# Turning C and a quarter of x by VectorE and transfers instead of TensorE, in a gated mix of an S5 layer and an FFN

## The chip, the cores and the metric

One core of a Trainium2 chip. The metric is the device time of one execution in microseconds (us), the median of several runs. Engines are called TensorE (PE in the profile), VectorE (DVE), ScalarE (ACT), GpSimd (POOL) and SyncE (SP); SP issues most transfers.

## What is computed

x is one sequence of 2048 tokens of 448 features, in bf16. Out of it come an S5 state space layer `a` and a dense FFN `b`, mixed by a gate of each token. `x = A_x` feeds both.

```
g    = sigmoid((x * gate_w).sum(-1))
a:     Lam_bar = exp(dt * Lam);  B_bar = ((Lam_bar - 1) / Lam) * Bmat        # complex, 448 states
       Bu = x @ B_bar.T;   h[t] = Lam_bar * h[t-1] + Bu[t]
       a  = 2 * real(h @ Cmat.T) + x * Dskip
b:     b  = silu(x @ w1) @ w2                                                # 448 -> 1792 -> 448
out  = g * a + (1 - g) * b
```

## The kernel before

**Tiling.** The 2048 tokens are worked on in four chunks `tc` of 512 (CH), each of four token tiles `tb` of 128. The 448 complex states are 896 real rows, held as 7 slots of 128 (slots 0 to 2 and the lower half of slot 3 real, the rest imaginary). The names of the products in the lists of work are:

- F(tc): x times w1, 14 tiles of 128 columns for each chunk; ScalarE applies silu while it copies PSUM to `aT` (L634).
- B(tc): x times B, 7 tiles for each chunk, copied out of PSUM to `U` (`UG`), by VectorE in the first chunk (L640) and by ScalarE in the others (L642).
- G(tb): the second FFN product, 14 matmuls (L774); ScalarE scales by 1 - g into `fe` (L780), and a GpSimd transfer adds that to `Tb` in SBUF (L782). `Tb` is `xnat` itself, in which x times Dskip times g already lies (L849).
- C(tb): the readout of 7 matmuls, state `H` times scaled `CP` (L795). VectorE computes g * product + `Tb` (L798), SP stores it (L801).

F and B (L663) run as pairs of 64-row matmuls, side by side, with one bank pair of PSUM for each pair of tiles; there are four bank pairs. They need x and B with features on partitions. x comes in with tokens on partitions (`xnat`) and is turned by TensorE with an identity matrix: `x0_transposes` for chunk 0 (L478), `x_transposes` for chunks 1 to 3 (32 small matmuls each, L508, copied out of PSUM at L516 and L518). B is turned in the same way (`b_transposes`, L604). C is loaded to `Cnat` (which shares its memory with H2), turned by TensorE in four groups (`readout_weights`, L814) and scaled out of PSUM by ScalarE (L822, L825) and VectorE (L827, L830) into `CP`.

**The recurrence** (`lanes(tc)`). VectorE rotates U by COS and SIN into `H` (A) with the help of `PI`, scans the seven slots (`tensor_tensor_scan`, L736) into the f32 buffer `Gf`, and rotates back into H with the help of `PO`. Between, `Gf` is cast to bf16 in `U` again, by GpSimd transfers (L390) in chunks 0 to 2 and by ScalarE in chunk 3 (L746). In chunk 0 the first rotation is 18 small operations, in the others four large ones (L729 to L732). There are two `UG`, one `PI`, `PO` and `Gf`, and four `H`.

**The order.** Operations are put into a `Plan`. TensorE's order is the one in which they are added: the last lines of the function write it out by hand. Every other engine's order comes from a list scheduler (`order`, L104): of the operations that could start earliest by its own costs it takes the one with the lowest `prio`. Loads are reckoned at 300 KB per us in the order of their queue (`RATE`, L60). The order is fixed when the kernel is built; on the chip each engine works through its list, and an instruction that waits holds up everything behind it on that engine. TensorE's list:

```
F0 (8 tiles), B0, F0 (6), B1; parameters, turning of B and of x chunk 1 in between
cp(0) G(0,1) cp(1,2) G(2,3) cp(3)
F1, F2 (1 tile), B2; x chunk 2 turned in between
G(4..7) C(0..3)
F2 (13), B3, F3; x chunk 3 turned in between
C(4..7) G(8..11) C(8..11) G(12..15) C(12..15)
```

**Loads.** SP issues x chunk 0, w1, the parameters, B, the last part of w1, gate_w and Dskip, x chunk 1, w2, C in eight pieces, and x chunks 2 and 3 (L401 to L441).

Of the kernel before, what the change touches and what calls it, by code (L numbers as in the profile page):

```python
# [7 lines left out]
ALU = mybir.AluOpType  # L8
# [6 lines left out]
S_TOK = 2048  # L15
# [9 lines left out]
NFILL = 2  # L25
XCOL = [0, 128, 256, 320]
# [22 lines left out]
class Op:  # L49
    __slots__ = ("i", "eng", "fn", "reads", "writes", "cost", "prio", "sem",  # L50
                 "deps", "succ", "ps_w", "ps_r", "start", "end", "bytes", "tag", "own")


class Plan:
# [5 lines left out]
    RATE = {"pool": 300e3, "hw": 300e3}  # L60
    LAP = {"dve": 0.08, "act": 0.09}
# [6 lines left out]
    def add(self, eng, fn, reads=(), writes=(), cost=0.2, prio=50, sem=None, nbytes=0, tag=""):  # L68
# [28 lines left out]
        o.own = False  # L97
        o.start = o.end = None
# [5 lines left out]
    def order(self):  # L104
# [14 lines left out]
        def earliest(o):  # L119
            t = 0.0  # L120
# [23 lines left out]
        while len(done) < len(ops):  # L144
# [5 lines left out]
            for eng, lst in cands.items():  # L150
# [9 lines left out]
                o = min((c for c in cand if c[0] <= t0 + 1e-9), key=lambda c: (c[1].prio, c[1].i))[1]  # L160
# [116 lines left out]
def bass_gated_mix__ssm_conv_s5__dense_activation_silu__prompt_kernel(nc, A_x, A_Lambda_re, A_Lambda_im, A_B_re, A_B_im, A_C_re, A_C_im,  # L277
               A_log_dt, A_Dskip, B_x, B_w1, B_w2, gate_w, out):
    with ExitStack() as ctx:
# [9 lines left out]
        xT = sb("xT", [128, 4, S_TOK], BF16)  # L289
# [3 lines left out]
        CP = sb("CP", [128, NSLOT, D_MOD], BF16)  # L293
        aT = [sb(f"aT{k}", [128, NFB, CH], BF16) for k in range(2)]
        UG = [sb(f"UG{k}", [128, 8, CH], BF16) for k in range(2)]
# [3 lines left out]
        H2C = sb("H2C", [128, 3840], BF16)  # L299
        H = [H2C[:, 0:3584].rearrange("p (s n) -> p s n", s=NSLOT) if k == 2 else sb(f"H{k}", [128, NSLOT, CH], BF16) for k in range(4)]  # L300
        Cnat = H2C[:, :].rearrange("p (b l) -> p b l", b=4)
        cnn = [f"H2_{s}" for s in range(7)] + ["H2_3i"]
# [91 lines left out]
        def load_w1(q, k, a, b):  # L394

            cols = slice(w1cuts[k], w1cuts[k + 1])
            src = B_w1[320:448, cols] if a == 3 else B_w1[128 * a:128 * b, cols].rearrange("(b p) f -> p b f", p=128)
            load(q, w1s[:, 3, cols] if a == 3 else w1s[:, a:b, cols], src, " ".join(f"w1_{k}_{i}" for i in range(a, b)),
                 256 * (b - a) * (cols.stop - cols.start))
# [11 lines left out]
        Bnat = H[3][:, :, 0:D_MOD]  # L411
        load("sp", Bnat[:, 0:3, :], A_B_re[0:384, :].rearrange("(b p) d -> p b d", p=128), "H3_0 H3_1 H3_2", 384 * 896)
        load("sp", Bnat[0:64, 3, :], A_B_re[384:448, :], "H3_3", 64 * 896)
        load("sp", Bnat[64:128, 3, :], A_B_im[384:448, :], "H3_3i", 64 * 896)
        load("sp", Bnat[:, 4:7, :], A_B_im[0:384, :].rearrange("(b p) d -> p b d", p=128), "H3_4 H3_5 H3_6", 384 * 896)
        btn = {s: [f"BT{s}_{h}" for h in range(2)] for s in range(7)}
        load_w1("sp", len(w1cuts) - 2, 0, 3)
        load_w1("sp", len(w1cuts) - 2, 3, 4)
# [8 lines left out]
        def load_C():  # L427

            for h in range(2):
                rows = lambda a: a[224 * h:224 * h + 224, :].rearrange("(b p) l -> p b l", p=56)  # L430
                to = Cnat[64 * h:64 * h + 56]
                load("sp", to[:, :, 0:448], rows(A_C_re), f"Cn0{h} " + (" ".join(cnn) if h == 0 else ""), 224 * 896)
                load("sp", to[:, :, 576:960], rows(A_C_im[:, 0:384]), f"Cn1{h}", 224 * 768)
                load("sp", to[:, :, 448:512], rows(A_C_im[:, 384:448]), f"Cn2{h}", 224 * 300)
                load("sp", to[:, :, 512:576], rows(A_C_re[:, 384:448]), f"Cn3{h}", 224 * 300)
# [32 lines left out]
        def x0_transposes(q0, part, who):  # L468
# [12 lines left out]
            for h in range(2):  # L481
                src = lambda h=h: bk(tk, h).bitcast(BF16)[:, 0:256].rearrange("p (q b n) -> p q b n", q=2, n=64)
                dst = xT[:, q0:q0 + 2, 256 * part:256 * part + 256].rearrange("p q (b h n) -> p q b h n", h=2, n=64)[:, :, :, h, :]
# [11 lines left out]
        xn_of = {tc: {q: [f"xT{tc}_{h}" for h in range(2)] for q in range(4)} for tc in range(1, NCH)}  # L495
        xn_of[0] = {q: [f"xT0_{q}{part}{h}" for part in range(2) for h in range(2)] for q in range(4)}

        def x_transposes(tc, who):
# [13 lines left out]
            for h in range(2):  # L512
                src = lambda h=h: bk(tk, h).bitcast(BF16).rearrange("p (q b n) -> p q b n", q=4, b=4)
                dst = xT[:, :, tc * CH:(tc + 1) * CH].rearrange("p q (b h n) -> p q b h n", h=2, n=64)[:, :, :, h, :]
                if who[h] == "d":
                    DVE(lambda e, src=src, dst=dst: e.tensor_copy(dst, src()), [tk], [f"xT{tc}_{h}"], 0.69, 2.2, "xTe")  # L516
                else:
                    ACT(lambda e, src=src, dst=dst: e.activation(dst, src(), AF.Copy), [tk], [f"xT{tc}_{h}"], act_cost(1024), 2.2, "xTe")  # L518

# [73 lines left out]
        def b_transposes(s0, s1, who):  # L593
# [12 lines left out]
            PE(mm, [f"H3_{s}" for s in range(s0, s1)] + ["H3_3i"] * (s0 <= 3 < s1) + ["ident"], [tk], n * 4 * 0.0285, "BT")  # L606
# [16 lines left out]
        def evict(pair, tk):  # L623

            kinds = [t[0] for t in pair]
            for k, n in ((0, 2),) if pair[0][:2] == pair[-1][:2] and len(pair) == 2 else ((0, 1), (1, 1))[:len(pair)]:
# [10 lines left out]
                U, un = UG[tc % 2], f"U{tc % 2}_"  # L637
                dst = U[:, sl, :]
                if tc == 0:
                    DVE(lambda e, src=src, dst=dst: e.tensor_copy(dst, src()), [tk], [f"{un}{m}" for m in names], 0.15 + 0.53 * n, 2.6, "U")  # L640
                else:
                    ACT(lambda e, src=src, dst=dst: e.activation(dst, src(), AF.Copy), [tk], [f"{un}{m}" for m in names], act_cost(512 * n), 5, "U")  # L642
# [4 lines left out]
        def x_products(tiles, fill={}, wait=()):  # L647
# [10 lines left out]
            def steps(k, h, a, z):  # L658
                def body(pe):
                    for n, cut in list(enumerate(part[h]))[a:z]:  # L660
                        for b, ((i, p0), tile) in enumerate(zip(cut, pairs[k])):
                            tc = tile[1]
                            r = pe.matmul(bk(toks[k], b), weights(tile, p0, p0 + 64, i), xT[p0:p0 + 64, i, tc * CH:(tc + 1) * CH],  # L663
# [42 lines left out]
        def lanes(tc):  # L706
            pr = 20 + tc
            A, an = H[tc], f"H{tc}"
            U, u = UG[tc % 2], f"U{tc % 2}_"
            Gb = U  # L710
            t = f"L{tc}"
            if tc == 0:
# [20 lines left out]
            for s in (3, 0, 4, 1, 5, 2, 6) if tc else (0, 4, 1, 5, 2, 6, 3):  # L733
# [8 lines left out]
                for dst, src, name in cuts:  # L742
                    if tc + 1 < NCH:
                        load("pool", dst, src, name, 180000, 1, [f"Gf{s}"])
# [23 lines left out]
        def ffn2(tb):  # L768
# [13 lines left out]
            P.add("pool", lambda e: e.dma_start(Tb[:, tb, :], f[:, :], accum_op=ALU.add), [fn, f"Tb{tb}"], [f"Tb{tb}"], 0.94, 2, sem(), 115000, tag="Tb+")  # L782

        outs = [sem() for _ in range(NOT)]

        def readout(tb):
# [3 lines left out]
            for n, (a, b) in enumerate(cuts):  # L790
                tk = Ps()

                def mm(pe, tk=tk, a=a, b=b):
                    for s in range(NSLOT):
                        r = pe.matmul(bk(tk)[:, 0:b - a], H[tc][:, s, o:o + 128], CP[:, s, a:b], start=(s == 0), stop=(s == NSLOT - 1))  # L795
                    return r
                PE(mm, [f"H{tc}_{s}" for s in range(7)] + [f"CP{s}" for s in range(NSLOT)], [tk], NSLOT * (0.0025 + (b - a) / 2400), f"C{tc}")
# [5 lines left out]

        def readout_weights(k):

            tk = Ps(2)

            def mm(pe):
                for j, c0 in ((0, 128 * k), (1, 448 if k == 3 else 576 + 128 * k)):
                    for b in range(4):  # L810
                        o = j * 224 + 56 * b
                        for h in range(2):
                            p = slice(64 * h, 64 * h + 56)
                            r = pe.transpose(bk(tk, h).bitcast(BF16)[:, o:o + 56], Cnat[p, b, c0:c0 + 128], ident[p, p])  # L814
                return r
            PE(mm, [f"Cn{n}{h}" for n in range(4) for h in range(2)] + cnn + ["ident"], [tk], 8 * 0.0285, "CT")
# [102 lines left out]
```

## Time and profile before

| what | value |
|---|---|
| median of 3 runs (lowest, highest) | 141.22 us (141.2, 141.76) |
| the profiled execution | 141.25 us, its span 139.5 us |
| granted TensorE clock | 0.998 |
| TensorE busy, matmuls | 135.9 us (97%), 1201 |
| VectorE busy | 122.0 us (87%) |
| ScalarE busy | 90.3 us (65%) |
| GpSimd busy | 39.2 us (28%) |
| read from HBM, written | 7.17 MB, 1.84 MB |

The span is the time from the first to the last instruction in the trace; the difference to the execution's time lies around it. Times in timelines are microseconds from the span's start, then the duration. A row of the chain gives start, length, engine, tile, line of the kernel and number of instructions. A row of the groups gives line, engine, operation, result and operands with shape, count, then busy time and mean duration in ns, then the idle time ahead of it. A row of the windows gives a stretch, its length, the busy time of TensorE's matmuls and weight loads, VectorE, ScalarE and GpSimd in it, each with its number of instructions, then the clock, the busy share of the 16 DMA engines and GB/s.

### The profile page before, as it was taken

How to read it: one execution, taken by the hardware profiler on the slowest of the kernel's cores; microseconds unless marked ns; L12 is line 12 of the kernel's file. 1: busy time of each engine (PE TensorE's matmuls, PEld its weight loads, DVE VectorE, ACT ScalarE, POOL GpSimd, SP SyncE). 2: the span in 40 equal slices, each digit the busy share in tenths (PEclk: the TensorE clock that was granted, in tenths of full speed). 3: DMA queues.
4: the chain of work that ended last, by engine and by line, in shares of the span. 5: the costliest groups of instructions: out<-in, count | busy, mean ns of one | idle time of the engine just before them, and what ended most of it. 6: DMA issues, size and time to landing. Idle time of an engine off the chain costs nothing.

```text
span 139.5 us, 3000 instructions
## 1 busy us (share of the span) xinstructions
PE 135.9 (97%) x1201; PEld 67.0 (48%) x1201; DVE 122.0 (87%) x179; ACT 90.3 (65%) x157; POOL 39.2 (28%) x72
## 2 busy tenths in 40 slices
PE   7999999999999999999999999999999999999992
PEld 2445454455544544455544544444455555555561
DVE  0319999999999999999999999999999999997053
ACT  3349768999989999823694887799931268312300
POOL 7134040100248440227733001824000314022220
PEclk9999999999999999999999999999999999999999
DMA  4998999510156770104976200674202322323242
GB/s 136 337 294 243 363 320 238 177 42 0 31 79 94 129 110 1 38 15 73 157 131 155 38 5 0 95 133 79 38 4 97 66 33 36 83 83 61 40 94 71
DMA packets 17956, 14.71 MB, mean 105 GB/s; under 512 B 2835, under 2 KB 17814, under 8 KB 17942
## 3 DMA queue, kind: packets, MB, share of 16 engines
q0 software_dynamic: 6064, 5.51, 24.8%
q1 hardware_dynamic: 11318, 8.65, 20.7%
q10 hardware_dynamic: 560, 0.36, 0.8%
q8 instruction: 9, 0.15, 0.4%
q14 instruction: 5, 0.04, 0.1%
HBM read 7.17 MB, written 1.84 MB: 65 GB/s over the span
## 4 chain that ended last, share of the span: by engine, by line
PE 97%; DVE 0%; issue 0%
PE ps L663 46%; PE ps L774 31%; PE ps L795 15%; PE ps L463 2%; PE ps L508 1%; PE ps L478 1%; PE ps L814 1%; PE ps L604 1%; DVE ot L798 0%; PE ps L675 0%; PE ps L464 0%; PE ps L536 0%
## 5 line engine op out<-in xcount | busy, mean ns | idle before, releaser
L663 PE MATMUL ps<-xT,w1s 64*128 64x512 bf16 x392 | 48.5, 378 | 0.0
L774 PE MATMUL ps<-w2s,aT 128*128 128x448 bf16 x224 | 43.2, 353 | 0.0
L634 ACT ACTIVATE aT<-ps 128x1024 bf16<-128x1024 f32 (+1 forms) x30 | 28.7, 969 | 8.5 <-PE ps L663 8.4
L774 PEld LDWEIGHTS ps<-w2s,aT 128*128 128x128 bf16 x224 | 21.7, 98 | 20.4 <-ACT xnat L849 0.4
L663 PEld LDWEIGHTS ps<-xT,w1s 64*128 64x128 bf16 x392 | 19.7, 94 | 22.3 <-DVE xT L486 0.7
L663 PE MATMUL ps<-xT,BT 64*128 64x512 bf16 x196 | 25.8, 376 | 0.0
L782 POOL DMA_DIRECT2D xnat<-fe x16 | 14.1, 900 | 37.9 <-ACT fe L780 37.2
L780 ACT ACTIVATE fe<-ps,g 128x448 bf16<-128x448 f32 x16 | 10.1, 632 | 21.1 <-PE ps L774 21.0
L390 POOL DMA_DIRECT2D UG<-Gf x27 | 14.7, 549 | 20.9 <-DVE Gf L736 20.4
L736 DVE TENSOR_TENSOR_SCAN Gf<-rc,gin,H 128x512 f32<-128x512 f32 x14 | 17.2, 1268 | 0.0
L795 PE MATMUL ps<-CP,H 128*128 128x448 bf16 (+2 forms) x98 | 16.4, 326 | 0.0
L663 PEld LDWEIGHTS ps<-xT,BT 64*128 64x128 bf16 x196 | 10.8, 94 | 11.1 <-DVE Gf L562 0.2
L798 DVE SCALAR_TENSOR_TENSOR ot<-ps,g,xnat 128x448 bf16<-128x448 f32 (+2 forms) x18 | 10.8, 622 | 6.0 <-issue 4.6
L390 POOL DMA_DIRECT2D UG<-UG x8 | 4.8, 597 | 29.2 <-ACT UG L642 17.4
L704 DVE TENSOR_TENSOR H<-UG,COS 128x3584 bf16<-128x3584 bf16 (+4 forms) x10 | 12.6, 1266 | 0.0
L795 PEld LDWEIGHTS ps<-CP,H 128*128 128x128 bf16 x98 | 8.9, 98 | 7.5 <-DVE k L752 0.4
L642 ACT ACTIVATE UG<-ps 128x1024 bf16<-128x1024 f32 (+1 forms) x12 | 10.7, 923 | 1.4 <-PE ps L663 1.4
L842 ACT ACTIVATE junk<-xg 128x448 bf16<-128x448 bf16 x16 | 9.2, 574 | 2.1 <-DVE xg L704 2.0
L849 ACT ACTIVATE xnat<-xnat,g 128x448 bf16<-128x448 bf16 x16 | 9.8, 671 | 0.2
L704 DVE TENSOR_TENSOR PI<-UG,SIN 128x512 bf16<-128x512 bf16 (+2 forms) x13 | 9.1, 722 | 0.0
L704 DVE TENSOR_TENSOR PO<-UG,SIN 128x1536 bf16<-128x1536 bf16 (+1 forms) x8 | 8.7, 1087 | 0.1
L736 DVE TENSOR_TENSOR_SCAN Gf<-rc,gin,H2C 128x512 f32<-128x512 f32 x7 | 8.5, 1265 | 0.0
(102 smaller groups left out, 126.5 us busy)
## 6 DMA issues: line engine op xcount, KB each, us to landing
UG<-Gf POOLq DMA_DIRECT2D x21, 128.0 KB, 2.5
xnat<-fe POOLq DMA_DIRECT2D x16, 112.0 KB, 2.6
out_dram<-ot SPq DMA_DIRECT2D x15, 112.0 KB, 1.7
w2s<-in_B_w_dram SPq DMA_DIRECT2D x1, 1568.0 KB, 11.8
xnat<-in_A_x_dram SPq DMA_DIRECT2D x3, 448.0 KB, 6.1
w1s<-in_B_w_dram SPq DMA_DIRECT2D x1, 576.0 KB, 6.2
UG<-UG POOLq DMA_DIRECT2D x8, 64.0 KB, 2.2
H2C<-in_A_C_re_dram SPq DMA_DIRECT2D x2, 196.0 KB
```

The source lines that it names most:

```text
L390: P.add(q, lambda e: e.dma_start(dst, src), list(after), name.split(), 0.6 if q == "pool" else 0.5, prio, sem(), nbytes, tag="ld " + name)
L634: ACT(lambda e, src=src, dst=dst: e.activation(dst, src(), AF.Silu), [tk, "tbl"], [f"aT{tc % 2}_{m}" for m in names], act_cost(512 * n), 2 ...
L642: ACT(lambda e, src=src, dst=dst: e.activation(dst, src(), AF.Copy), [tk], [f"{un}{m}" for m in names], act_cost(512 * n), 5, "U")
L663: r = pe.matmul(bk(toks[k], b), weights(tile, p0, p0 + 64, i), xT[p0:p0 + 64, i, tc * CH:(tc + 1) * CH], start=(h == 0 and n == 0), stop=( ...
L704: DVE(lambda e: e.tensor_tensor(o, a, b, op), r, w, dve_cost(n, 2), prio, tag)
L736: DVE(lambda e, s=s, b=b, init=init: e.tensor_tensor_scan(Gf[:, s, :], rc[:, b:b + 1].to_broadcast([128, CH]), A[:, s, :], init, ALU.mult, ...
L774: r = pe.matmul(bk(tk)[:, 0:D_MOD], aT[tc % 2][:, fb, o:o + 128], w2s[:, fb, :], start=(fb == 0), stop=(fb == NFB - 1))
L780: ACT(lambda e: e.activation(f[:, :], bk(tk)[:, 0:D_MOD], AF.Copy, scale=g1[:, tb:tb + 1]), [tk, f"g1_{tc}"], [fn], act_cost(448, 1), 7, "fe")
L782: P.add("pool", lambda e: e.dma_start(Tb[:, tb, :], f[:, :], accum_op=ALU.add), [fn, f"Tb{tb}"], [f"Tb{tb}"], 0.94, 2, sem(), 115000, tag= ...
L795: r = pe.matmul(bk(tk)[:, 0:b - a], H[tc][:, s, o:o + 128], CP[:, s, a:b], start=(s == 0), stop=(s == NSLOT - 1))
L798: DVE(lambda e, tk=tk, a=a, b=b: e.scalar_tensor_tensor(ot[tb % NOT][:, a:b], bk(tk)[:, 0:b - a], g[:, tb:tb + 1], Tb[:, tb, a:b], ALU.mul ...
L849: ACT(lambda e, tb=tb: e.activation(Tb[:, tb, :], xnat[:, tb, :], AF.Copy, scale=g[:, tb:tb + 1]), [f"xd{tc}", f"g_{tc}"], [f"Tb{tb}"], ac ...
```

## The change

- **C** is loaded ahead of w2 instead of behind it, in six pieces, with rows in plain order (128 x 3 and 64 x 1); GpSimd clears the last block before. `readout_columns` turns it by four VectorE transposes of 32x32 blocks into `C32` (which lies in UG2), and 16 SP transfers carry the blocks to their places in `CP`. The scaling of `CP` then works in place on SBUF.
- **x's last chunk** is turned in the same way by `x_blocks(3)`: four VectorE transposes into X32 (which lies in H2), and 16 SP transfers into `xT`, whose layout becomes chunk by chunk. Chunks 1 and 2 are still turned by TensorE, chunk 1 one pair of tiles earlier (`XT1K`).
- **Bu copies** of chunk 0: slots 0, 1, 4, 5 stay with VectorE, slots 2, 3 and 6 go to ScalarE.
- **Eight f32 sums**: for tiles 4 to 11 the readout is scaled by ScalarE into f32 `ct`, a GpSimd transfer adds it to `Tb`, and SP stores `Tb`.
- **Buffers**: three `UG` and three `H`, each used by `tc % 3`; B comes in through UG2.
- **Order**: the first lanes use the four large operations. C(0..3) stands behind the third block of products, lanes(3) behind C(0..3), and G(12,13) ahead of C(8..11). Gates, scaling and transposes get priorities of their own, and the planner's reckoned transfer sizes change.

The core of the diff:

```diff
+L0M = True
+XT1K = 6
+XPRIO = {2: 15, 3: 20.2}
+XBLK = (3,)
+UDVE = (0,1,4,5)
+OUTA = tuple(range(4,12))
+CPRIO = 2.9
+CPP = 20.5
+CTAT = 59.0
+GPR = (14, 20.3, 21.5, 19)
...
-        UG = [sb(f"UG{k}", [128, 8, CH], BF16) for k in range(2)]
+        UG = [sb(f"UG{k}", [128, 8, CH], BF16) for k in range(3)]
...
+        H = [sb(f"H{k}", [128, NSLOT, CH], BF16) for k in range(3)]
+        Cnat = H[2][:, :, :].rearrange("p s n -> p (s n)").rearrange("p (b l) -> p b l", b=4)
...
+            for b0, b1, p in ((0, 3, 128), (3, 4, 64)):
+                rows = lambda a: a[128 * b0:128 * b0 + p * (b1 - b0), :].rearrange("(b p) l -> p b l", p=p)
+                for dst, src in (((0, 448), rows(A_C_re)), ((512, 896), rows(A_C_im[:, 0:384])), ((448, 512), rows(A_C_im[:, 384:448]))):
...
         load_xn(1)
+        load_C()
         load("sp", w2s[:, :, :], B_w2.rearrange("(fb p) d -> p fb d", p=128), "w2", F_FF * 896)
-        load_C()
...
+        def x_blocks(tc):
+            X32 = (xT[:, 3, :, :] if tc == 2 else H[2][:, 0:4, :]).rearrange("p m (q b i) -> p m q b i", q=4, i=32)
...
+            for k, (q0, q1, c, b0, b1) in enumerate(((0, 3, 0, 0, 2), (0, 3, 0, 2, 4), (3, 4, XCOL[3], 0, 2), (3, 4, XCOL[3], 2, 4))):
+                n = q1 - q0
+                src = xs[:, b0:b1, c:c + 128 * n].rearrange("p b (q m i) -> p b q m i", q=n, i=32)
+                dst = X32.rearrange("p m q b i -> p b q m i")[:, b0:b1, q0:q1, :, :]
+                DVE(lambda e, dst=dst, src=src: e.transpose(dst, src), [f"xn{tc}"] + names[0:k][0:1], [names[k]] + cnn * (tc == 3 and k == 0), 0.15 + 256 * n / 960, XPRIO[tc], "xTd")
+            k = sem()
+            for g in range(4):
+                for m in range(4):
+                    to = xT[32 * m:32 * m + 32, tc, :, :].rearrange("p q (b g i) -> p (q b) g i", b=4, i=32)[:, :, g, :]
+                    P.add("sp", lambda e, to=to, g=g, m=m: e.dma_start(to, X32[32 * g:32 * g + 32, m, :, :, :].rearrange("p q b i -> p (q b) i")),
+                          names + held, [f"xT{tc}_{g}{m}"], 0.68, 400, k, 150000, tag="xTm")
...
-                if tc == 0:
+                if tc == 0 and a in UDVE:
...
+                if tb in OUTA:
+                    f, fn = ct[tb // 2 % 2][:, tb % 2, :], f"ct{tb // 2 % 2}{'ab'[tb % 2]}"
+                    ACT(lambda e, tk=tk, f=f: e.activation(f, bk(tk)[:, 0:D_MOD], AF.Copy, scale=g[:, tb:tb + 1]),
+                        [tk, f"g_{tc}"], [fn], act_cost(448, 1), 3, "out")
+                    P.add("pool", lambda e, f=f: e.dma_start(Tb[:, tb, :], f, accum_op=ALU.add), [fn, f"Tb{tb}"], [f"Tb{tb}"], 0.94, 2, sem(), 300000, tag="Tb+")
+                    P.add("sp", lambda e: e.dma_start(out2[t0:t0 + 128, :], Tb[:, tb, :]), [f"Tb{tb}"], [], 0.3, 1, outs[NOT], 128 * 896, tag="st")
+                    continue
...
+        def readout_columns():
+            C32 = UG[2][:, 0:NSLOT, :].rearrange("p s n -> p (s n)").rearrange("p (m t b i) -> p m t b i", m=4, b=4, i=32)
...
+            for b in range(4):
+                src = Cnat[:, b, :].rearrange("p (t m i) -> p t m i", m=4, i=32)
+                dst = C32.rearrange("p m t b i -> p b t m i")[:, b, :, :, :]
+                DVE(lambda e, dst=dst, src=src: e.transpose(dst, src), [f"Cn{n}" for n in range(6)] + ["Cnz"] + [CBEH] * (CBEH != "") + cnn + turned, [names[b]],
+                    0.15 + 896 / 960, CPRIO, "CTd")
...
+                    to = CP[32 * m:32 * m + 32, :, :].rearrange("p t (b g i) -> p (t b) g i", b=4, i=32)[:, :, g, :]
+                    P.add("sp", lambda e, to=to, g=g, m=m: e.dma_start(to, C32[32 * g:32 * g + 32, m, :, :, :].rearrange("p t b i -> p (t b) i")),
+                          names + held, [f"CT{g}{m}"], 0.75, 400, k, 300000, tag="CTm")
...
-        for f in cp(0) + G(0, 1) + cp(1, 2) + G(2, 3) + cp(3):
+        for f in G(0, 1, 2, 3):
             f()
-        x_products(F(1) + F(2, 0, 1) + B(2), {2: xt(2, "aa")})
+        for f in cp(0, 1, 2, 3):
+            f()
+        x_products(F(1) + F(2, 0, 1) + B(2), {2: xt(2, "aa")} if 2 not in XBLK else {})
...
-        for f in G(4, 5, 6, 7) + C(0, 1, 2, 3):
+        for f in G(4, 5, 6, 7):
             f()
-        x_products(F(2, 1) + B(3) + F(3), {1: xt(3, "aa"), 9: [lambda: gates(3), lambda: lanes(3)]})
-        for f in C(4, 5, 6, 7) + G(8, 9, 10, 11):
+        x_products(F(2, 1) + B(3) + F(3), {1: xt(3, "aa") if 3 not in XBLK else [], 9: [lambda: gates(3)]})
+        for f in C(0, 1, 2, 3):
             f()
-        for f in C(8, 9, 10, 11) + G(12, 13, 14, 15) + C(12, 13, 14, 15):
+        lanes(3)
+        for f in C(4, 5, 6, 7) + G(8, 9, 10, 11, 12, 13) + C(8, 9, 10, 11) + G(14, 15) + C(12, 13, 14, 15):
             f()
```

More of the change, by code (lines that the diff above doesn't have):

```diff
@@ L50 @@
     __slots__ = ("i", "eng", "fn", "reads", "writes", "cost", "prio", "sem",
-                 "deps", "succ", "ps_w", "ps_r", "start", "end", "bytes", "tag", "own")
+                 "deps", "succ", "ps_w", "ps_r", "start", "end", "bytes", "tag", "own", "at")
 class Plan:
@@ L802, in readout @@
                       [f"ot{tb % NOT}{n}"], [], 0.3, 1, outs[tb % NOT], 128 * 2 * (b - a), tag="st")
[L804 to L820 removed]
+        ctn = [f"CT{g}{m}" for g in range(4) for m in range(4)]
@@ L826, in readout_weights @@
                 both.append(cn + "b")
-            DVE(lambda e: e.scalar_tensor_tensor(in_two(CP[:, k, :]), re(), sc1[:, k:k + 1], in_two(c[:, 0, :]), ALU.mult, ALU.add),
-                [tk, "sc1"] + both, [f"CP{k}"], 0.68, 1, "CP")
+            else:
+                for a, b in ((slice(0, 64), slice(64, 128)), (slice(64, 128), slice(0, 64))):
+                    ACT(lambda e, a=a, b=b: e.activation(c[a, 0, :], CP[b, 3, 0:D_MOD], AF.Copy, scale=sc2[b, 3:4]), ctn + ["sc2"], [cn + "a"], act_cost(448, 1), 8, "ct").at = CTAT
```

123 lines of the change are left out of this document (71 added, 52 removed).

## The prediction

> **What bounds the kernel now.** I read the page's first two parts, then the chain that ended last in order of time, then each engine's timeline against that chain.
>
> ```profile
> PE 135.9 (97%) x1201; PEld 67.0 (48%) x1201; DVE 122.0 (87%) x179; ACT 90.3 (65%) x157; POOL 39.2 (28%) x72
> ...
> DVE  0319999999999999999999999999999999997053
> ...
> PE 97%; DVE 0%; issue 0%
> ```
>
> TensorE is busy almost all the time and the chain that sets the end is TensorE from front to back. VectorE is second: full from slice 4 to slice 36. So a microsecond taken from TensorE is worth a microsecond as long as VectorE keeps up. The chain gives the stages:
>
> ```profile
> 28.31 0.21 PE ps L814 x16
> 28.51 5.40 PE ps L774 x28
> 33.92 0.52 PE ps L814 x32
> ...
> 39.84 0.31 PE ps L814 x16
> ...
> 57.24 10.70 PE ps L774 x56
> 67.94 5.30 PE ps L795 x28
> 73.24 3.99 PE ps L663 x36
> 77.23 0.47 PE ps L508 x32
> 77.70 21.80 PE ps L663 x202
> ...
> 104.90 10.59 PE ps L774 x56
> ...
> 131.38 5.35 PE ps L795 x42
> ```
>
> The pieces follow each other without a gap (left out are repeats: two token tiles of L774 always take 5.4 us, a chunk of four 10.6, a chunk of L795 5.3). L814 turns C, L508 turns x, L774 is the second FFN product, L795 the readout, L663 the products with x.
>
> How near is VectorE? The last readout, at 131.38, needs the last state chunk, whose last VectorE pair is this:
>
> ```profile
> 126.07 2.09 DVE L704 TENSOR_TENSOR H<-H,PO 128x2048 bf16<-128x2048 bf16 x2
> ```
>
> It ends at 128.16, so VectorE is 3.2 us early at 131.38. It has no idle time worth naming before that, so whatever it is given or relieved of earlier arrives there one for one. That 3.2 us is the second number of this prediction.
>
> **The change, part by part.**
>
> *TensorE.* The four C groups go: 0.21 + 0.52 + 0.31 = 1.04 us. The turning of x's last 512 tokens goes: 0.47 us. Sum 1.51 us; the other products stay. C(0..3) moves behind F(3), and G(12), G(13) before C(8..11): reordered, not shortened. The new stages, each row's length kept: G(0..3) ends at 39.1, F(1)+F(2,0)+B(2) at 56.2, G(4..7) at 66.9, the third x block at 92.7, C(0..3) at 98.0, C(4..7) at 103.3, G(8..13) at 119.2, C(8..11) at 124.5, G(14,15) at 129.87; C(12..15) starts there instead of at 131.38.
>
> *VectorE, removed.*
>
> ```profile
> L798 DVE SCALAR_TENSOR_TENSOR ot<-ps,g,xnat 128x448 bf16<-128x448 f32 x15 | 9.9, 673 | 5.9 <-issue 4.6 <-PE ps L795 1.3
> L640 DVE CAST UG<-ps 128x1024 bf16<-128x1024 f32 x3 | 3.6, 1216 | 0.0
> L640 DVE CAST UG<-ps 128x512 bf16<-128x512 f32 x1 | 0.7, 682 | 0.0
> L704 DVE TENSOR_TENSOR PI<-UG,SIN 128x512 bf16<-128x512 bf16 x7 | 2.7, 416 | 0.0
> L704 DVE TENSOR_TENSOR H<-H,PI 128x512 bf16<-128x512 bf16 x7 | 2.7, 414 | 0.0
> L704 DVE TENSOR_TENSOR H<-UG,COS 128x1024 bf16<-128x1024 bf16 x3 | 2.0, 683 | 0.0
> L704 DVE TENSOR_TENSOR H<-UG,COS 128x512 bf16<-128x512 bf16 x1 | 0.4, 412 | 0.0
> ```
>
> Eight readouts: 8 x 0.673 = 5.38 us. Two Bu copies, one of each form: 1.22 + 0.68 = 1.90 us. The first lanes' 18 small operations (7 x 0.416 + 7 x 0.414 + 3 x 0.683 + 0.412 = 8.27 us) become the four large ones that the other lanes use; these are in the timeline:
>
> ```profile
> 51.89 2.02 DVE L704 TENSOR_TENSOR H<-UG,COS 128x3584 bf16<-128x3584 bf16 x1
> 53.82 1.22 DVE L704 TENSOR_TENSOR PO<-UG,SIN 128x2048 bf16<-128x2048 bf16 x1
> 54.96 0.95 DVE L704 TENSOR_TENSOR PI<-UG,SIN 128x1536 bf16<-128x1536 bf16 x1
> 55.82 2.02 DVE L704 TENSOR_TENSOR H<-H,PO 128x3584 bf16<-128x3584 bf16 x1
> ```
>
> Together 6.21 us, so 2.06 us less. All removed: 9.34 us.
>
> *VectorE, added.* Four transposes of 896 columns, two of 768, two of 256. No row shows one. The cheapest near row is an SBUF copy, the dearest the scan:
>
> ```profile
> L565 DVE COPY COS<-COS 128x1536 bf16<-128x1536 bf16 x1 | 0.5, 531 | 0.0
> L736 DVE TENSOR_TENSOR_SCAN Gf<-rc,H 128x512 f32<-128x512 f32 x7 | 8.1, 1200 | 0.0
> ```
>
> By the copy (0.35 ns per column) the 5632 columns cost 2.0 us, by the scan (2.34 ns) 13.2 us. I take the rate of the CAST above, one element of each partition at a time: (1216 - 682) / 512 = 1.04 ns per column and 0.15 us to start, so 1.08, 0.95 and 0.42 us, 7.1 us in all. Net by durations -2.3 us. But consecutive VectorE operations overlap (51.89 + 2.02 runs past 53.82, by 0.09 us), and 16 fewer instructions lose that 16 times: about 1.3 us back. Net -1.0 us: the last state is done at 127.2, against a need at 129.87. Margin 2.7 us, before any new wait.
>
> [...]
>
> *The new wait on C.* C's transposes wait on VectorE until C has landed, and behind them in its queue stand Bu copies, the x copy and the phase work. C now takes w2's place in the load queue, and w2 follows.
>
> ```profile
> L390 SPq DMA_DIRECT2D w2s<-in_B_w_dram x1: 507/507/507, 10.1 to 10.1; - x1
> ...
> DMA to landing us min/median/max: 11.8/11.8/11.8
> ```
>
> ```profile
> 16.00:19.00 3.00, 3.00 (x30) 1.36 (x28) 3.00 (x5) 1.25 (x3) 0.50 (x1) 1.00 1.09 380
> 20.00:23.50 3.50, 3.50 (x42) 1.63 (x36) 3.50 (x9) 3.03 (x5) 0.09 (x1) 1.00 1.02 211
> ```
>
> w2 landed at 21.9. Its 1568 KB take 4.2 us at 380 GB/s; C's 0.80 MB take 2.1 us, and 448 short packets about 1 us. So C lands between 18.5 and 21 (21.9 - 4.2 + 3.2). The planner in the code reckons 300 KB per us in queue order, 4.66 MB, and so 18 us. VectorE therefore stands idle 0.5 to 3 us near 19; I take 1.5. TensorE does not notice: four bank pairs of 1.5 us each lie between a pair's end and its reuse. Margin left at 129.87: 1.2 us. And w2: pushed back by C's 3 us, it lands by 25, or 23 if its own tail was C's doing; G(0) needs it at 28.3. Cost nothing; without that cover, the lateness one for one.
>
> *The moves.* C32 is carried to CP in 16 transfers of 32 partitions in runs of 32 bf16, 64 bytes: 14,336 packets (16 x 32 x 28). x needs 16 x 32 x 16 = 8,192. The trace has no 64-byte run. The last stores have short ones: 128 of 896 bytes, 128 of 384, twice 128 of 256.
>
> ```profile
> 136.90:137.40 0.50, 0.00 (x0) 0.00 (x0) 0.20 (x1) 0.00 (x0) 0.00 (x0) 1.00 0.67 228
> ...
> 137.90:138.35 0.45, 0.00 (x0) 0.00 (x0) 0.00 (x0) 0.00 (x0) 0.00 (x0) 1.00 0.33 73
> ```
>
> That is 0.67 x 0.5 x 16 / 128 = 42 ns per 896-byte packet and 0.33 x 0.45 x 16 / 128 = 18.6 ns per 256-byte packet. A straight line through both gives 12 ns at 64 bytes. From above, while C landed in 128-byte pieces:
>
> ```profile
> DMA packets 1384, 0.74 MB, mean 211 GB/s; under 512 B 694, under 2 KB 1359, under 8 KB 1384
> ```
>
> In that window (20 to 23.5) the 16 engines were busy 57 us together, and 0.74 MB at the rate of 16 to 19 takes 34; putting the rest on the 694 short ones gives 39 ns each with their own bytes. Range 12 to 39; I take 18.6, the nearest row. Then C's moves hold all 16 engines for 16.7 us (10.8 to 35), x's for 9.5 us (6 to 20). Their neighbours:
>
> ```profile
> 28.00:57.00 29.00, 29.00 (x310) 14.15 (x306) 28.91 (x46) 28.20 (x56) 9.68 (x16) 1.00 0.38 61
> 54.32 0.59 ACT L642 ACTIVATE UG<-ps 128x512 bf16<-128x512 f32 x1
> 60.96 2.02 DVE L704 TENSOR_TENSOR H2C<-UG,COS 128x3584 bf16<-128x3584 bf16 x1
> ```
>
> Other transfers need 0.38 x 29 = 11 us of that stage. With the C transposes done near 24.5, C's moves are over by 52 and x's by 62. C32 lies in UG2, which ScalarE overwrites with B(2) first at 54.3 - 1.0 = 53.3: hidden, narrowly. x's blocks must be in xT by 77 and out of H2 by lanes(2), near 61: hidden for the first, a wait of a microsecond at most for the second, where lanes(1) has scans to do. The scaled C is not needed before 92.7; its ScalarE and VectorE work is the same as before. SP issues the 32 moves in a stretch where its queue has nothing else until the first store.
>
> *Sums, copies, buffers.* Eight readouts on ScalarE (0.63 us each, as fe) and eight accumulating transfers on POOL (0.9 us each) fall into the last 45 us, where both engines have room (98 to 129: ACT 13.67, POOL 5.11 of 31 us). The last of these stores is ready near 130, ahead of the last four. ScalarE takes 1.6 us of Bu copies and gives 2 us of x copies. H0 is reused: lanes(3) must wait for C(0..3) until 98.0, but its 20.7 us of VectorE work (start 96.35 in the old order with the readouts between) need not begin before 107. All at nothing.
>
> ```profile
> 98.00:129.00 31.00, 31.00 (x171) 15.82 (x168) 30.00 (x35) 13.67 (x23) 5.11 (x6) 1.00 0.26 55
> ```
>
> **Sum.** The profiled execution took 141.25 us (span 139.5 and 1.75 around it); the median shown is 141.22, so no correction. 141.25 - 1.51 = **139.7 us**, -1.1%. About 0.5% (0.7 us) is what a measurement of this kernel can tell from no change.
>
> **The rivals.**
>
> 1. *VectorE takes the bound and eats the gain.* Same mechanism, two sizes. For it: only 1.2 us of margin left, and 1.5 us of guessed waiting in it. If waits and dearer transposes come 2.0 to 3.4 us above my sum, the gain of 1.51 shrinks to within 0.5%: 140.5 to 141.9. Against it: the other terms are rows.
>
> 2. *VectorE ends on the other side.* The price is the transposes'. From 2.7 us above my sum the kernel is slower than before; by the scan's rate it is 6.1 us above, 4.9 past the margin: 144.6 us. The place is the wait of the first of C(12..15). Against it: a transpose has one input and no carried state, as the CAST and not as the scan.
>
> 3. *The moves are too slow.* From about 25 ns per packet C's moves end after 57.8 (24.5 + 11 + 22.3), which is 53.3 plus three bank pairs of 1.5 us; then ScalarE's B(2) copy waits, and TensorE behind it. At 30 ns: 62.4, 4.6 us lost, 144.3. At 39 ns it would be 12 us. For it: the 128-byte pieces of C. Against it: the 256-byte stores. [...] The stores show a short packet cheaper than a long one, though not in proportion.
>
> 4. *The turning was not on the path.* If TensorE then waits for w2 or for evictions in place of the removed work, some of the 1.51 us comes back: 140.5 to 141.3. Little speaks for it: the chain has no gap at those groups.
>
> **Chances.** Forecast 0.62 (its own range 139.3 to 140.5); rivals 1 and 4 together 0.16; rival 2, 0.12; rival 3, 0.10. Of rivals 1 and 4 some 0.02 stays faster by over 0.5% and 0.02 turns slower. So faster 0.64, same 0.12, slower 0.24. For 8 in 10 the range runs from 139.2 into the near half of rivals 2 and 3: 142.8.
>
> **What would show it.** Right: no L814, and L508 with 64 matmuls, TensorE still gapless, C(12..15) starting near 129.9. Transposes near 1.08 us for 896 columns. VectorE idle once near 19, by 0.5 to 3 us. The C moves landed before 53, with no ScalarE wait at the B(2) copies. Wrong: a TensorE gap ahead of C(12..15) (rival 1 or 2), a ScalarE wait on a transfer near 53 (rival 3), a gap at the first L774 (rival 4).

## The result, and the profile after

| | kernel before | changed kernel |
|---|---|---|
| median of 6 runs (lowest, highest) | 141.36 us (141.18, 143.53) | 140.56 us (140.29, 140.75) |
| ratio, 95% interval | | 0.9942 (0.9922 to 0.9962) |
| the profiled execution, its span | 141.25 us, 139.5 us | 140.58 us, 138.1 us |
| around the span | 1.75 us | 2.48 us |

The kernel is faster, by 0.6% where 1.1% was forecast: 0.8 us instead of 1.5. Means and counts of executions further down leave out single executions that took over 1.5% more than the fastest of their kernel. The first parts of the page after the change:

```profile
span 138.1 us, 2837 instructions
...
PE 133.9 (97%) x1105; PEld 65.4 (47%) x1105; DVE 120.9 (88%) x163; ACT 95.4 (69%) x166; POOL 46.8 (34%) x81
```

TensorE lost 2.0 us of busy time and 96 matmuls, VectorE 1.1 us. The chain that ended last (start, length, engine, tile, line, instructions; L819 is the second FFN product, L840 the readout, L708 the products with x, L533 the turning of x):

```profile
17.88 0.47 PE ps L533 x32
...
28.06 10.70 PE ps L819 x56
...
44.26 0.47 PE ps L533 x32
...
129.62 3.99 PE ps L840 x21
...
134.30 0.67 DVE ot L850 x2
```

x is turned twice instead of three times, no group turns C, and no piece before the last readouts belongs to another engine than TensorE. G(0) starts at 28.06 and C(12..15) at 129.62; the forecast was 129.87. So the stage that the change was to shorten is as short as forecast. VectorE's timeline (start, length, engine, line, operation) answers the next steps:

```profile
20.01 4.09 DVE L867 STREAM_TRANSPOSE UG<-H 128x896 bf16<-128x896 bf16 x4 [0.20 <-ACT xT L543]
...
125.03 2.09 DVE L749 TENSOR_TENSOR H<-H,PO 128x2048 bf16<-128x2048 bf16 x2
```

VectorE stood idle for 0.20 us ahead of C's transposes, and the trace puts that down to ScalarE's copy of `xT`, not to C: C's last piece landed at 19.79, when VectorE's operation before was just over (19.80). The last state was done at 127.12, 2.5 us before its readout. SP's timeline shows the 32 moves:

```profile
24.12 13.60 SPq L873 DMA_DIRECT2D CP<-UG  x16
46.65 12.07 SPq L561 DMA_DIRECT2D xT<-H  x16
```

The DMA view of 46.65 to 61.00, where x's moves lie, shows what their packets took (packets, MB, share of 16 engines):

```profile
q1 hardware_dynamic: 8448, 0.53, 33.9%
```

0.339 x 14.35 us x 16 engines / 8448 packets = 9.2 ns for a packet of 64 bytes. What paced the moves was not the packets but SP, with 0.85 us for each issue of C and 0.75 us for each of x; the 16 DMA engines were 68% busy in both stretches. A move of C landed 2.9 us after its issue (the page's median), the last one at 40.7, and the first copy of B(2) into the buffer did not wait:

```profile
52.82 0.64 ACT L687 ACTIVATE UG<-ps 128x512 bf16<-128x512 f32 x1
```

On TensorE everything up to the last readout went as forecast. The missing half lies behind it. Here are SP's last stores after the change, from its timeline:

```profile
134.79 0.43 SPq L853 DMA_DIRECT2D out_dram<-ot  x1
135.69 0.33 SPq L853 DMA_DIRECT2D out_dram<-ot  x1
136.07 0.42 SPq L853 DMA_DIRECT2D out_dram<-ot  x1
```

The first of these ends at 135.22 and the next begins at 135.69, though its data were there at 134.97 (the readout of 134.30 and 0.67). In this hole of 0.47 us SP does nothing that the trace shows. And around the span lie 2.48 us instead of 1.75.

### The profile page after: what moved, and what is told of

Read it like the earlier page. It is cut to its first block, busy times and chain, and to the rows that moved or that the text cites. A ratio compares the mean times of both kernels' runs of the same rounds, so it can differ in the third digit from the quotient of the medians.

```text
span 138.1 us, 2837 instructions
## 1 busy us (share of the span) xinstructions
PE 133.9 (97%) x1105; PEld 65.4 (47%) x1105; DVE 120.9 (88%) x163; ACT 95.4 (69%) x166; POOL 46.8 (34%) x81
## 3 DMA queue, kind: packets, MB, share of 16 engines
HBM read 7.11 MB, written 1.84 MB: 65 GB/s over the span
## 4 chain that ended last, share of the span: by engine, by line
PE 93%; DMA 3%; DVE 1%; ACTq 1%; issue 0%; DVEq 0%
PE ps L708 46%; PE ps L819 31%; PE ps L840 14%; DMA w1s<-in_B_w_dram 3%; DVE ot L850 1%; ACTq L407 1%; PE ps L533 1%; PE ps L648 1%; PE ps L580 0%; DVEq L289 0%
## 5 line engine op out<-in xcount | busy, mean ns | idle before, releaser
L708 PE MATMUL ps<-xT,w1s 64*128 64x512 bf16 x392 | 47.8, 376 | 0.2 <-DMA w1s<-in_B_w_dram 0.2
L819 PE MATMUL ps<-w2s,aT 128*128 128x448 bf16 x224 | 43.0, 353 | 0.0
L819 PEld LDWEIGHTS ps<-w2s,aT 128*128 128x128 bf16 x224 | 21.8, 98 | 20.9 <-issue 0.8
L708 PEld LDWEIGHTS ps<-xT,w1s 64*128 64x128 bf16 x392 | 19.9, 94 | 22.6 <-issue 0.8
L708 PE MATMUL ps<-xT,BT 64*128 64x512 bf16 x196 | 25.8, 376 | 0.0
L781 DVE TENSOR_TENSOR_SCAN Gf<-rc,gin,H 128x512 f32<-128x512 f32 x21 | 25.5, 1267 | 0.0
L407 POOL DMA_DIRECT2D UG<-Gf x27 | 15.3, 622 | 19.4 <-DVE Gf L781 19.2
L840 PE MATMUL ps<-CP,H 128*128 128x448 bf16 (+2 forms) x126 | 21.7, 332 | 0.0
L840 PEld LDWEIGHTS ps<-CP,H 128*128 128x128 bf16 x126 | 11.6, 98 | 10.0 <-DVE xg L749 0.4
L749 DVE TENSOR_TENSOR H<-UG,COS 128x3584 bf16<-128x3584 bf16 (+2 forms) x9 | 16.2, 1811 | 0.0
L708 PEld LDWEIGHTS ps<-xT,BT 64*128 64x128 bf16 x196 | 10.8, 94 | 11.2 <-DVE Gf L606 0.2
L687 ACT ACTIVATE UG<-ps 128x1024 bf16<-128x1024 f32 (+1 forms) x14 | 12.3, 903 | 0.5 <-PE ps L708 0.5
L850 DVE SCALAR_TENSOR_TENSOR ot<-ps,g,xnat 128x448 bf16<-128x448 f32 (+2 forms) x10 | 5.6, 582 | 5.2 <-issue 4.3
L749 DVE TENSOR_TENSOR PI<-UG,SIN 128x1536 bf16<-128x1536 bf16 (+1 forms) x8 | 8.5, 1083 | 0.0
L749 DVE TENSOR_TENSOR H<-H,PO 128x3584 bf16<-128x3584 bf16 (+2 forms) x5 | 8.1, 1644 | 0.0
```

What stands on the lines that cost most here:

```text
L407: P.add(q, lambda e: e.dma_start(dst, src), list(after), name.split(), 0.6 if q == "pool" else 0.5, prio, sem(), nbytes, tag="ld " + name)
L749: DVE(lambda e: e.tensor_tensor(o, a, b, op), r, w, dve_cost(n, 2), prio, tag)
L781: DVE(lambda e, s=s, b=b, init=init: e.tensor_tensor_scan(Gf[:, s, :], rc[:, b:b + 1].to_broadcast([128, CH]), A[:, s, :], init, ALU.mult, ...
L819: r = pe.matmul(bk(tk)[:, 0:D_MOD], aT[tc % 2][:, fb, o:o + 128], w2s[:, fb, :], start=(fb == 0), stop=(fb == NFB - 1))
L840: r = pe.matmul(bk(tk)[:, 0:b - a], H[tc % 3][:, s, o:o + 128], CP[:, s, a:b], start=(s == 0), stop=(s == NSLOT - 1))
```

## The experiments

The first four runs ask whether the 1.5 us of TensorE came in full and were lost behind the last readout, and what the parts are worth. All four, with runs of the kernel before between them, were made on one chip.

### The two kernels again (r_before, r_after)

No edit.

> The kernel before, once more, for more executions with their spans. Theory A (TensorE's path is shorter by the forecast 1.5 us in every execution of the changed kernel, and what is missing lies behind the last readout and around the span) expects spans of 139.4 to 139.6 us and 1.7 to 1.8 us around them. Theory B (something inside the span gives back 0.6 us in most executions, and the profiled one was a lucky one) expects the same here; this run is the base.

> The changed kernel, once more. Both theories: 140.3 to 140.8 us, 0.5 to 0.9 us under the kernel before. Theory A: the chain again reaches the first of C(12..15) near 129.6 and the last VectorE operation near 135.3, whatever the execution; spans of 138.1 and of 138.7 differ in the stores or ahead of the first instruction. Theory B: in an execution with a span of 138.6 or more, TensorE has a gap or a late start that this trace shows, and C(12..15) starts after 130.0.

Measured: the kernel before against itself 0.9999 (0.9973 to 1.0024); the changed kernel 0.9932 (0.9906 to 0.9958). In these two profiled executions the first load landed at the same moment, so their chains can be laid side by side. The chain of the kernel before, whose span is 139.8 us:

```profile
6.16 3.02 PE ps L663 x26
...
131.74 5.35 PE ps L795 x42
...
137.11 0.35 DVE ot L798
```

That of the changed kernel, whose span is 138.8 us:

```profile
6.16 2.98 PE ps L708 x26
...
130.19 3.99 PE ps L840 x21
...
135.56 0.35 DVE ot L850
```

C(12..15) starts 131.74 - 130.19 = 1.55 us earlier (forecast 1.51), and VectorE's last operation ends 137.46 - 135.91 = 1.55 us earlier. But from there to the end of the span it is 139.8 - 137.46 = 2.34 us before and 138.8 - 135.91 = 2.89 us after. The span therefore shrinks by 1.0 us. Around the span, the kernel before takes 1.75 to 1.87 us in 27 executions (mean 1.81), the changed kernel 1.75 to 2.90 in 11 (mean 2.02). -1.55 + 0.55 + 0.21 = -0.8 us. The first result was 0.8 us, and the ratio of this run is worth 1.0 us (0.6 to 1.3), so the sum fits within the noise.

The last stores of the kernel before, and then those of the changed kernel, from SP's timeline:

```profile
136.89 0.43 SPq L801 DMA_DIRECT2D out_dram<-ot  x1
137.37 0.45 SPq L801 DMA_DIRECT2D out_dram<-ot  x1
137.86 0.43 SPq L801 DMA_DIRECT2D out_dram<-ot  x1
```

```profile
135.36 0.43 SPq L853 DMA_DIRECT2D out_dram<-ot  x1
136.24 0.33 SPq L853 DMA_DIRECT2D out_dram<-ot  x1
136.62 0.42 SPq L853 DMA_DIRECT2D out_dram<-ot  x1
```

Before, the last three are 0.48 and 0.49 us apart; after, there are 0.88 us between the first two of the three. The hole is there again, ahead of the same store. A further run of the changed kernel (r_after2: 0.9922, 0.9893 to 0.9952) has it too, 0.89 us between the same two stores.

### x's last chunk by TensorE again (x3_by_tensor)

```diff
-XBLK = (3,)
+XBLK = ()
```

> x's last 512 tokens turned by TensorE as before, C still by VectorE. The prediction's step: 0.47 us of TensorE come back, VectorE is relieved of 2.7 us. Theory A: 0.4 to 0.5 us longer than the changed kernel, all of it on TensorE's chain. Theory B (the gain is lost in waits that the moves make): no longer than the changed kernel, or shorter.

Measured: 0.9974 (0.9948 to 0.9999), in the mean 0.5 us more than the changed kernel. TensorE's third group is back in the chain:

```profile
71.39 0.47 PE ps L533 x32
```

The size is as expected, 0.47 us, but the comparison is less clean than it looks. This kernel has 16 moves fewer in SP's list and no hole there, and around the span it takes 1.76 to 1.87 us in 10 executions; yet one of VectorE's last readouts began 0.4 us late, after 1.02 us of waiting where its neighbours wait 0.64. The chain shows where the time went; "issue" is time in which VectorE waited for nothing that the trace shows:

```profile
134.88 0.41 issue
135.29 0.15 DVE ot L850
```

One loss went and another came, and the second looks like the first: a pause of 0.41 us, this time on VectorE.

### Without the f32 sums (no_f32_sums)

```diff
-OUTA = tuple(range(4,12))
+OUTA = ()
```

> No f32 sums: VectorE does the eight readouts 4 to 11 again, 8 x 0.60 us ahead of the last state. VectorE was 2.5 us early at C(12..15) in the changed kernel. If that margin is what the prediction took it for, 4.8 - 2.5 = 2.3 us longer than the changed kernel, with a TensorE gap ahead of C(12..15). The rival (VectorE has hidden room, its order makes the margin): under 0.5 us longer. If the eight stores of the sums are what lengthens the end, the stretch from the last VectorE operation to the end of the span falls from 2.8 to 2.4 us.

Measured: 1.0261 (1.0230 to 1.0291), some 4.4 us above the changed kernel, where 2.3 were expected. VectorE has its eight readouts back and finishes the last state at 132.09, 4.3 us later than in r_after (127.75); its timeline, and TensorE's:

```profile
130.01 2.08 DVE L749 TENSOR_TENSOR H<-H,PO 128x2048 bf16<-128x2048 bf16 x2
```

```profile
132.16 7.19 PE L840 MATMUL ps<-CP,H 128*128 128x448 bf16 x42 [1.99 <-DVE H L749]
```

So VectorE's margin is real, and the sums bought it: without them TensorE waits 1.99 us. That is the expected part. The rest is that C(12..15) then took 7.19 us instead of the 5.35 of L795 above. The windows show why (stretch, length, TensorE, weight loads, VectorE, ScalarE, GpSimd, then the granted clock):

```profile
133.00:134.00 1.00, 1.00 (x5) 0.34 (x4) 0.00 (x0) 0.00 (x0) 0.00 (x0) 0.50 0.30 42
...
135.00:136.00 1.00, 1.00 (x4) 0.44 (x3) 0.35 (x1) 0.00 (x0) 0.00 (x0) 0.50 0.00 0
136.00:137.00 1.00, 1.00 (x7) 0.50 (x6) 0.25 (x1) 0.00 (x0) 0.00 (x0) 1.00 0.33 115
```

Within a microsecond after the gap the granted clock fell to 0.50, and it stayed there to 136. A gap of 2 us cost nearly 4 in the traced execution. One of the other five has a mean granted clock of 1.000 and is as slow, with a span of 143.2 us; no trace shows why.

The expectation also asked whether the eight stores of the sums lengthen the end. They do not: without them 0.46 us lie empty between the same two of the last stores (139.60 to 140.06), and from VectorE's last operation to the end of the span it is 142.7 - 139.74 = 3.0 us.

### Chunks 2 and 3 of x by VectorE (x23_by_vector)

```diff
-XBLK = (3,)
+XBLK = (2, 3)
```

> The changed kernel with chunk 2 of x turned by VectorE and moved too (16 more SP transfers). TensorE loses another 0.47 us; VectorE gets about 2.4 us more against a margin of 2.5 us at the first of C(12..15). Theory C: SP's list is 16 longer, so the hole is gone too: 0.9 to 1.2 us under the changed kernel if the margin holds. If VectorE is late by more than the margin, TensorE has a gap ahead of C(12..15) and the time is over the changed kernel's, by the gap and by what a gap of 2 us cost in the run without f32 sums: as much again at half the clock.

Measured: 1.0349 (1.0293 to 1.0406); the execution with the profile took 149.4 us, the others 146.3 to 148.1. The expectation missed the mechanism. TensorE's waits, then the chain:

```profile
PE ps L708 <- DMA xT<-xT: 5.4, 1, 5.4
```

```profile
52.24 1.80 SPq L561
...
54.09 2.67 DMA xT<-xT
...
56.80 9.05 PE ps L708 x58
```

It was not VectorE's margin that ran out. The moves of chunk 2 stand in SP's queue behind C's and begin at 39.05; the last lands at 56.76, 5.4 us after TensorE wanted the chunk. Then TensorE ran at a clock of 0.50 for some 4 us more (0.50 from 56 to 60, 0.69 in the mean of 60 to 62, 1.00 behind that). Up to 46.6 SP issues a move every 0.75 us. The next five issues take 1.1 to 1.8 us, and these moves land 5.0 us after their issue (the median). The DMA view of 46.6 to 54.1 shows the engines full, by the GpSimd transfers of the scan (q0) more than by the moves (q1):

```profile
q0 software_dynamic: 1041, 0.95, 87.8%
q1 hardware_dynamic: 2634, 0.16, 27.6%
```

Here TensorE does wait for moves, as in rival 3 of the prediction, but not because a 64-byte packet is dear (0.276 x 7.5 us x 16 / 2634 = 12.6 ns): the moves start late behind C's, go at SP's pace, and their last six meet the scan's transfers. No run separates these three.

### What makes the hole: sixteen more waits (sp_pad, sp_pad2)

Theory C: the 32 moves and their waits lengthen SP's list of instructions, so that a pause at a fixed place of that list, which in the kernel before falls where nobody waits, now falls between the last stores. Rival D: the changed kernel's last stores are slower for a reason of their own (the new stores of `Tb` have just been ruled out as that reason). Waits on a semaphore that has long been reached take SP little time but lengthen the list: the instructions that close its list with waits take 0.02 to 0.03 us each in the trace of the changed kernel, and one of them holds two waits. They are put ahead of SP's first store:

```diff
...
+first = next(i for i, it in enumerate(W.lists["sp"]) if it[0] == "do" and it[1] is first_store)
+W.lists["sp"][first:first] = [("wait", W.tl["pool"], 1)] * 32
```

> The changed kernel with 16 more wait instructions on SP ahead of its first store (each on a semaphore that has long reached its value). Theory C (the 32 moves lengthen SP's list so that the place where it must fetch instructions falls between its last two stores: a hole of 0.45 us there, and up to 1 us behind the last instruction): the hole between the last two issues goes, the stretch around the span is 1.8 us in all executions, and the time is 0.5 to 0.8 us under the changed kernel's. Rival D (the end is longer because of what the stores wait for or carry): no difference beyond 0.2 us.

> The changed kernel with 16 waiting instructions more in SP's list, once more and with more rounds, to tell its time from the changed kernel's, which the first interval did not. Theory C: ratio 0.988 to 0.991 to the kernel before, 0.4 to 0.5 us below the changed kernel; no hole between the last stores. Rival D: ratio 0.993, as the changed kernel.

Measured: 0.9889 (0.9836 to 0.9941) and 0.9916 (0.9883 to 0.9949). SP's last stores in the first of the two:

```profile
135.64 0.43 SPq L853 DMA_DIRECT2D out_dram<-ot  x1
136.12 0.46 SPq L853 DMA_DIRECT2D out_dram<-ot  x1
136.62 0.43 SPq L853 DMA_DIRECT2D out_dram<-ot  x1
```

They are 0.48 and 0.50 us apart: the hole is gone. Against D, the work is the same and so are the stores. The mean time of the 11 executions is 140.5 us against 140.9 in 22 of the changed kernel, 0.4 us less; the intervals of the ratios overlap, so that this difference alone is likely, not certain. In both, the mean span is shorter (138.6 and 138.35 against 138.9). The time around the span is not mended: 1.83 us in the mean of the first, 2.22 in the second, with single executions up to 2.99.

### The same hole made in the kernel before (before_pad, before_pad31, before_pad29)

Theory C must work in the kernel before as well, which has no moves. Its list gets 66, 62 or 58 waits in the same place, which makes 33, 31 or 29 instructions.

```diff
...
+W.lists["sp"][first:first] = [("wait", W.tl["pool"], 1)] * 66
```

> The kernel before with 33 more wait instructions on SP ahead of its first store, so that its list is as long as the changed kernel's. Theory C: a hole of 0.4 to 0.5 us between the last stores, 0.4 to 0.8 us longer than the kernel before. Rival D: the same time as the kernel before, within 0.2 us.

> The kernel before with 31 waiting instructions more in SP's list (33 gave a hole of 0.45 us one store too early to be compared with the changed kernel, and no time that could be told from none). Theory C (the lengthened list of SP puts a hole of about 0.45 us at a fixed place of that list): two instructions fewer move the hole by one store, so that it lies between the third and the second store from the end, as in the changed kernel; the span's tail behind VectorE's last operation grows from 2.34 to about 2.8 us, and the time by 0.3 to 0.6 us against the kernel before. Rival D (the changed kernel's stores are slower for a reason of their own): no hole, and no time.

> The kernel before with 29 waiting instructions more in SP's list. Theory C: the hole moves by one store more, to just ahead of the last store, or behind it; ahead of it the tail grows by 0.4 to 0.5 us and the time by 0.3 to 0.6 us; behind it only what lies around the span can grow. Rival D: neither a hole nor a longer time.

With 33, the ratio is 1.0005 (0.9976 to 1.0034), with 31 it is 1.0050 (1.0027 to 1.0073), with 29 it is 0.9987 (0.9972 to 1.0003). SP's last stores with 33, with 31 and with 29 (the last two alone):

```profile
136.34 0.33 SPq L801 DMA_DIRECT2D out_dram<-ot  x1
137.12 0.33 SPq L801 DMA_DIRECT2D out_dram<-ot  x1
...
137.97 0.53 SPq L801 DMA_DIRECT2D out_dram<-ot  x1
```

```profile
136.82 0.43 SPq L801 DMA_DIRECT2D out_dram<-ot  x1
137.29 0.46 SPq L801 DMA_DIRECT2D out_dram<-ot  x1
138.17 0.33 SPq L801 DMA_DIRECT2D out_dram<-ot  x1
```

```profile
137.44 0.45 SPq L801 DMA_DIRECT2D out_dram<-ot  x1
137.93 0.43 SPq L801 DMA_DIRECT2D out_dram<-ot  x1
```

With 33 instructions the hole stands ahead of the third store from the end (0.45 us from 136.67 to 137.12), with 31 ahead of the last (0.42 us from 137.75 to 138.17), with 29 between no stores. Two instructions fewer move it on by two stores, so a store is one instruction, and the hole keeps its place in the list; the expectation for 31 was off by one store. Counting all of SP's instructions in the traces makes the place exact. In all eight traces in which the hole can be seen it lies between SP's 79th and 80th instruction: the 80th is the last store but one in after, r_after, r_after2 and no_f32_sums, the third from the end in before_pad, the last in before_pad31, a closing wait behind the stores in before_pad29 (0.44 us, 138.43 to 138.87), and a move of x in x23_by_vector (0.43 us, 66.88 to 67.31). In the two padded changed kernels the 80th is the first store, which waits for its data until 96.7. The kernel before has 54 instructions there and x3_by_tensor 71, so the place does not exist.

What the hole costs can be read from VectorE's last operation to the end of the span: 2.7 to 3.0 us in the six traces with the hole between the stores, 2.3 to 2.5 us in the other seven. Ahead of the last store it costs its whole length in the time too: the ratio's interval is worth 0.4 to 1.0 us, and two instructions fewer take that away again. Ahead of the third from the end, the profiled execution of before_pad has 2.7 us instead of 2.3, but the ratio's interval (-0.3 to 0.5 us) allows anything from nothing to that; the 0.4 to 0.8 us expected were not found in the time.

So it is shown that the length of SP's list makes the hole and that a hole ahead of the last store costs about its own length or a little more. What SP does in it is not seen, but a packet stands behind it. The page counts the packets of the queues that it calls "instruction"; here are those of q14 in the kernel before and in the changed kernel:

```profile
q14 instruction: 5, 0.04, 0.1%
```

```profile
q14 instruction: 6, 0.05, 0.1%
```

Every kernel whose SP list reaches 80 instructions has six, the kernel before and x3_by_tensor have five. The packet that is new starts 1.0 to 1.4 us after the end of SP's 79th instruction in all ten such traces, wherever that lies; it is of 8 KB. VectorE's pause in x3_by_tensor is followed by one as well, 0.70 us after its end. By its place and its queue's name the author takes such a packet for a refill of the engine's instructions; since SP's packet starts only when the hole is over, it cannot itself be what SP waits for; what that is was not shown.

## Why the prediction was half right

**Right, with their sizes.** TensorE: -1.51 forecast, -1.55 measured between r_before and r_after. C(12..15) at 129.87 forecast, 129.62 in the profile (1.76 us earlier than in the profile before; the pair whose first loads land together gives 1.55, so some 0.2 us of this belong to the execution and not to the change). VectorE's last state: 127.2 forecast before any new wait, 127.12 in the profile. w2: by 25 forecast, landed at 25.4; G(0) started at 28.06, without a wait. Sums, copies and buffers at nothing: no wait shows for them, and no_f32_sums shows that VectorE's margin of 2.5 us would be gone without the sums.

**The transposes.** The row chosen for a price, the CAST's 1.04 ns per column and 0.15 us, gave 1.08, 0.95 and 0.42 us. By groups, VectorE took:

```profile
L867 DVE STREAM_TRANSPOSE UG<-H 128x896 bf16<-128x896 bf16 x4 | 4.1, 1080 | 0.2 <-ACT xT L543 0.2
L556 DVE STREAM_TRANSPOSE H<-xnat 128x768 bf16<-128x768 bf16 x2 | 1.9, 967 | 0.0
L556 DVE STREAM_TRANSPOSE H<-xnat 128x256 bf16<-128x256 bf16 x2 | 0.9, 432 | 0.0
```

1.08, 0.97 and 0.43 us: the CAST's price.

**Right in the end, wrong in size.** The wait for C: 1.5 us taken, none that the trace shows, since VectorE was busy until C had landed (19.8, within the 18.5 to 21 forecast). So the margin was 2.5 us and not the 1.2 that the prediction was left with. The packets: 18.6 ns taken with 12 to 39 as bounds, 9.2 measured, below both. That the moves did not finish sooner still has another reason: the prediction gave SP's issuing no price, and it was the pace, 13.60 us for C's 16. It did no harm here, since C's moves had until 53. In x23_by_vector, where a second set of moves followed at once, it is part of what broke.

**The step that failed.** The sum ended with "141.25 - 1.51": the stretch behind the last readout and the 1.75 us around the span were carried over unchanged. Just before, the prediction let SP issue the 32 moves "in a stretch where its queue has nothing else". Both looked at when SP is busy and not at what else 32 more issues change: the place of the last stores in SP's list. The two terms that were taken as nothing are +0.55 us behind VectorE's last operation and +0.2 us in the mean around the span. The first is the hole, by sp_pad, before_pad31 and before_pad29: 0.40 of the 0.55 us stand in the gap between the stores (0.88 instead of 0.48). The second stays open in its cause: executions with more than 1.9 us around the span come in the changed kernel, in sp_pad, sp_pad2 and no_f32_sums, none in the kernel before, the padded kernels before, x3_by_tensor or x23_by_vector. The first four kernels have one thing in common, TensorE's 1105 matmuls; the others have 1201, 1137 or 1073. And the three profiled executions with the long stretch (after, r_after, no_f32_sums: 2.48 to 2.70 us) have a packet of an instruction queue 1.7 to 1.9 us behind the span's end, which none of the other ten has. This is the changed kernel's, in the window 138.2 to 142:

```profile
q8 instruction: 1, 0.02, 1.6%
```

The author's guess is a pause of the same sort on TensorE, by the length of its list; no run tested it.

**The rivals.** None of the four came about: no gap of TensorE ahead of C(12..15), transposes at the CAST's price, no wait for the moves, no gap at the first L819. A fifth was missing, the end of the kernel, which no rival named although every microsecond of it counts in full.

**A version ahead of both.** The changed kernel with 16 idle waits, sp_pad, is at 0.989 and 0.992 of the kernel before in its two runs: in the means 1.2 to 1.4 us of the 1.5.

## What to carry to other kernels

When work moves from an engine to transfers, count the issues twice: their time on the issuing queue (here 0.75 to 0.85 us each for moves of 64-byte runs, which set the pace and not the packets), and their place in that engine's list of instructions. Follow the chain past the last compute instruction: here SP issued the last stores one after the other, 0.48 and 0.49 us apart in r_before, a pause of 0.42 us ahead of the last one (before_pad31) lengthened the kernel by 0.4 to 1.0 us, and the spacing of the last stores in the timeline shows it at once. Padding the list with a few waits that are already met is a cheap way to tell such a pause from a slow store.

## What the runs showed of the hardware

- A pause of 0.42 to 0.47 us sits ahead of the 80th of SP's instructions in the trace, whatever that instruction is, and a packet of 8 KB on an instruction queue follows it. Ahead of the last store (before_pad31) it lengthened the kernel by about its own length (0.4 to 1.0 us by the ratio of 1.0050); ahead of a store that had to wait for its data anyway (sp_pad) or behind the last store (before_pad29, 0.9987) it cost nothing that can be seen.
- A 1.99 us gap of TensorE (no_f32_sums) was followed by a granted clock of 0.77 in the mean of 132.10 to 133.00 and of 0.50 from there to 136.00, and C(12..15) took 7.19 us instead of 5.35, 1.84 us more.
- VectorE's 32x32 block transposes took 1.08 us for 896 columns of bf16, the price of a copy that casts from f32 (0.15 us and 1.04 ns per column, by the two CAST rows of the kernel before).
- Transfers within SBUF in runs of 64 bytes took 9.2 ns per packet and engine, half of the 18.6 ns worked out for the stores' packets of 256 bytes. By the packet the 64 bytes are cheaper, by the byte they are twice as dear (0.14 against 0.07 ns).
- With the 16 DMA engines full (46.6 to 54.1 in x23_by_vector, 87.8% of q0 and 27.6% of q1), an issue on SP took up to 1.80 us instead of 0.65, and landing 5.0 us (the median).
